# Routing attention and a tanh-shrink MLP on one core: the first batch's pairs readied two pairs ahead, the weight conversion in two stages, the up-projection handed out in single products

## The chip, the cores and the metric

The kernel runs on one core of a Trainium2 chip. The metric is the device time of one execution in microseconds (us), and for several executions their median.

## The reference

```python
# B=4 batches, H=8 heads, S=768, D=64, 16 clusters; d_model 512, d_ff 2048
q_assign = argmax(einsum('bhsd,hcd->bhsc', q_n, c_n))      # the same for k
mask = q_assign[:, :, :, None] == k_assign[:, :, None, :]
scores = where(mask, q @ k.T / sqrt(D), -1e9)
attn = softmax(scores) @ v
x = attn.transpose(0, 2, 1, 3).reshape(B * S, H * D)
h = x @ w_in
out = (h - tanh(h)) @ w_out
```

The weights arrive as float64. The kernel reads them as pairs of 32-bit words and makes float32 of them on the chip.

## The kernel before, in words

**Attention.** The heads are taken in pairs, four pairs to a batch, 16 pairs n = 0 to 15. A pair takes six steps (two halves of the queries, three slices of the keys each), so there are 96 steps, 24 to a batch. In the loop, step `at` issues `begin` of the step after it (score products, tile `sc`, L371, then the exponential on ACT, tile `e`) and `value` of its own (`av`, L424; in the first batch also the sums `den` by products with ones, L433). Everything else of the step is put on a list `todo`, which `between()` empties in pieces after each matrix product of the MLP.

**The mask.** Before a pair can begin, it must be readied (`before`, the table `PLACES`): `turn` (six transposes of q and six of k, `pt`, L264), `similar` (`sim`, L282), `route` (`pr`, L295, and four DVE instructions that find the cluster), `publish` (`pq`, L322, a copy `qc` on DVE, L326, and a DMA of the codes to DRAM), `spread` (a DMA that copies the codes to all partitions, tile `row`), and for pairs below `MASKED` = 4 `one_hot` (two DVE instructions, L352 and L356). For these pairs the mask is then added by four bf16 products a step (L382). For the others DVE selects by `e` = (row == code) * sc, four instructions a step (L402), which also free the score buffers. The readying of pair n stands in the six steps of pair n-1 and one before, at places -1, 0, 0, 2, 3, 4.

**The weights.** During the first batch the list `makers` is worked off: 32 pieces of 512 KB are fetched by POOL's queue (tile `raw`, five ahead), converted (`assemble`: one ACT instruction for the low words, tile `rest`, L136; three DVE instructions for the high words, L137, L141, L144, into tile `unit`), combined into the factors of a seven-product Strassen scheme (`sum_of`, L550), and written to DRAM (`keep`, tensors `up_factors` and `down_factors`). There are eight units of four pieces and four sums.

**The MLP.** Batch b's MLP (`strassen_items`) fills the steps of batch b+1; that of the last batch runs alone at the end. It has eight `up_pair` items (seven products each, tile `pu`, L649, with the additions to `G` and `u` on DVE, L634, tanh on ACT, and subtractions on POOL, L639) and 21 `down_product` items (tile `pd`, L693). An item is given a weight (9.1 and 3.4), and a step takes whole items until its share of the weight is reached.

Of the kernel before, what the change touches and what calls it, by code (L numbers as in the profile page):

```python
# [38 lines left out]
P = 128  # L39
# [13 lines left out]
MASKED = 4  # L53
# [5 lines left out]
def kernel(  # L59
# [67 lines left out]
    def assemble(dst, raw, rest):  # L127

        bits = dst.bitcast(U32)
        pair = raw.rearrange("p (n two) -> p n two", two=2)
        lo, hi = pair[:, :, 0], pair[:, :, 1]
        if len(dst.shape) == 3:
            lo, hi, rest = (t.rearrange("p (a b) -> p a b", a=dst.shape[1]) for t in (lo, hi, rest))
        nc.scalar.activation(out=rest, in_=lo, func=ACT.Copy, scale=2.0**-29)  # L136
        nc.vector.tensor_scalar(  # L137
            out=bits, in0=hi, scalar1=3, scalar2=0x3FFFFFF8,
            op0=ALU.logical_shift_left, op1=ALU.bitwise_and,
        )  # L140
        nc.vector.scalar_tensor_tensor(  # L141
            out=bits, in0=hi, scalar=0xC0000000, in1=bits, op0=ALU.bitwise_and, op1=ALU.bitwise_or
        )
        nc.vector.tensor_tensor(out=bits, in0=bits, in1=rest, op=ALU.add)  # L144

    def fast():
# [4 lines left out]
        codep = cx.enter_context(tc.tile_pool(name="codep", bufs=3))  # L151
# [12 lines left out]
        first, AHEAD = ExitStack(), 5  # L164
        xin = first.enter_context(tc.tile_pool(name="xin", bufs=HP))
        unitp = first.enter_context(tc.tile_pool(name="unitp", bufs=2))
        rawp = first.enter_context(tc.tile_pool(name="rawp", bufs=AHEAD))
        restp = first.enter_context(tc.tile_pool(name="restp", bufs=2))
# [90 lines left out]
        def turn(n: int, i: int, engine):  # L259
# [8 lines left out]
            t = turned[n, i] = turnp.tile([P, 2, TB], F32, name=f"t{i}")  # L268
# [63 lines left out]
        def spread(n: int):  # L332

            if masked(n):
                t = rows[n] = rowp.tile([P, 2, 2, TB], BF16, name="row")
# [5 lines left out]
            else:  # L341
                t = rows[n] = rowp.tile([P, 2, 2, TB], BF16, name="row")
# [149 lines left out]
        units = {}  # L492

        def sources(m: int):

            up, q_, r = m < HF // 2, m % 4 // 2, m % 2
            if up:
                t = units[m] = unitp.tile([P, FQ, 8, P], F32, name="unit")
# [5 lines left out]
            t = units[m] = unitp.tile([P, 8, 2, HM], F32, name="unit")  # L504
            made = []
            for o in range(2):
                f = q_ * FQ + 2 * r + o
                made.append((t[:, 0:8:7, o], w_out_r[:, f]))
                made.append((t[:, SLOT[2] : 7 : SLOT[3] - SLOT[2], o], w_out_r[:, f + HF]))
            return made  # L510

        raws, queue = {}, []

        def fetch(at: int):
            m, i = at // 4, at % 4
            if m >= 8:
                return
            if i == 0:
                queue.extend(sources(m))
# [6 lines left out]

        def round_piece(at: int):
            if words == 2:
                rest = restp.tile([P, FQ * P], U32, name="rest")
                assemble(queue[at][0], raws.pop(at), rest)  # L530
            fetch(at + AHEAD)

        def sum_of(m: int, k_: int):
            t = units[m]
            up = m < HF // 2

            def part(which):
                return t[:, :, which] if up else t[:, which]
# [6 lines left out]
                ) if up else (  # L545
# [6 lines left out]
        def keep(m: int):  # L552
            t, q_, r = units.pop(m), m % 4 // 2, m % 2
            if m < HF // 2:
# [4 lines left out]
            else:  # L559
                f = q_ * FQ + 2 * r  # L560
                nc.sync.dma_start(
                    down_factors[:, :, f : f + 2].rearrange("k p i m -> p k (i m)"),
                    t[:, 0:7].rearrange("p k i m -> p k (i m)"),
                )

        makers = []
        for m in range(8):
            makers += [lambda at=4 * m + i: round_piece(at) for i in range(4)]

            makers.insert(len(makers) - 2, lambda m=m: keep(m - 1) if m else None)  # L570
            makers += [lambda m=m, k_=k_: sum_of(m, k_) for k_ in range(4)]
        makers += [lambda: keep(7)]
# [15 lines left out]
        late_pools, diffs = {}, {}  # L588

        def open_late():  # L590
            first.close()
            for name, bufs in (
                ("diff", 1), ("u", 2), ("s", 2), ("th", 2), ("g", 1), ("left", 1), ("du", 1), ("c", 4),
                ("raw", 3),
            ):
                late_pools[name] = cx.enter_context(
                    tc.tile_pool(name=name + "_late", bufs=bufs, reuse_waits="tile")
                )
            late_pools["G"] = late_pools["g"].tile([P, HF, 2, 2, TB], F32, name="G")
            late_pools["S1"] = late_pools["left"].tile([P, HF, TB], F32, name="S1")  # L600
# [16 lines left out]
        def strassen_items(b: int):  # L617
            base = b * PER

            def up_pair(i: int, between):  # L620
# [7 lines left out]
                }  # L628
                s = late_pools["s"].tile([P, TB], F32, name="s")
                u = late_pools["u"].tile([P, 2, TB], F32, name="u")  # L630
                g, left1 = late_pools["G"][:, i], late_pools["S1"][:, i]
# [13 lines left out]
                for k_, which in enumerate(PRODUCTS):  # L645
                    ps = ps_f.tile([P, TB], F32, name="pu", tag="f")
                    for c in range(CH):
                        for r in halves:
                            nc.tensor.matmul(  # L649
                                ps[r], lhsT=streams[base + i][:, c, k_, r], rhs=right[which][c],  # L650
                                start=(c == 0), stop=(c == CH - 1),
                            )
                    if which == 1:
                        nc.scalar.copy(out=s, in_=ps)
                        fetch_factors(base + i + 2)
                    elif which == 2:
                        add(g[:, 0, 0], ps, s)
                    elif which == 6:
                        add(u[:, 0], ps, s)
                    elif which == 7:  # L660
                        add(u[:, 1], ps, u[:, 0])
                    elif which == 4:
                        add(g[:, 1, 0], ps, u[:, 1])
                    elif which == 5:
                        add(u[:, 0], ps, u[:, 0])
                        add(g[:, 1, 1], ps, u[:, 1])
                        shrink(1)
                    else:
                        add(g[:, 0, 1], ps, u[:, 0])
                        shrink(0)  # L670
                    between()

                nc.gpsimd.tensor_tensor(out=left1, in0=g[:, 0, 1], in1=g[:, 1, 1], op=ALU.add)
                nc.gpsimd.tensor_tensor(out=g[:, 0, 1], in0=g[:, 0, 0], in1=g[:, 0, 1], op=ALU.subtract)
                streams.pop(base + i)
# [136 lines left out]
        for i in range(AHEAD):  # L812
            fetch(i)
# [302 lines left out]
```

## Time and profile before

| what | value |
|---|---|
| median of 3 runs | 1080.9 us (1079.85 to 1081.64) |
| the profiled execution | 1073.9 us, span 1072.1 us |
| mean granted clock of TensorE | 0.979 of full speed |
| TensorE (PE) busy | 1001.2 us, 93% of the span |
| VectorE (DVE) busy | 604.1 us, 56% |
| GpSimd (POOL) busy | 571.7 us, 53% |
| ScalarE (ACT) busy | 297.2 us, 28% |

The time that the runs show is some 7 us above that of the profiled execution, so a difference that is worked out from the trace is put on the median as it is. PE is busy nearly all the time; the table does not show where it is not, nor where it is busy at half its clock.

### The profile page before, as it was taken

To read this page: it belongs to the slowest core of one execution; us is meant where nothing else is said; L and a number is where in the kernel's file an instruction comes from. 1 tells how busy PE (TensorE), PEld (TensorE's weight loads), DVE (VectorE), ACT (ScalarE), POOL (GpSimd) and SP (SyncE) were. 2 spreads that over 40 slices of the span, in tenths; PEclk is the share of its full clock that TensorE was granted. 3 is DMA by queue.
4 is the path that set the end of the run, shared out by engine and by line. 5 is a ranking of instruction groups with operands and counts; after the bars stand their busy time and mean duration, and the time that the engine had idled before them with its cause. 6 is when DMAs were issued, how large, how long until landed. Compare 5 with 4: busy or idle time off the path is not lost.

```text
span 1072.1 us, 17120 instructions
## 1 busy us (share of the span) xinstructions
PE 1001.2 (93%) x6820; PEld 500.3 (47%) x6820; DVE 604.1 (56%) x1103; ACT 297.2 (28%) x447; POOL 571.7 (53%) x423
## 2 busy tenths in 40 slices
PE   7986978998999999999999999999899999999996
PEld 5432433343445555434335555444345555444664
DVE  5767869666645556766556545755455544644011
ACT  2543434233232212332242222322332121122000
POOL 1111212575779545575768536576668645456701
PEclk8998989999999999999999999999999999999998
DMA  8756776444353534434353323313212212322320
GB/s 236 232 177 224 252 230 212 172 137 124 134 176 116 189 132 160 153 116 138 128 161 104 127 71 123 90 69 113 90 59 95 89 51 93 113 92 108 118 95 32
DMA packets 92183, 142.85 MB, mean 133 GB/s; under 512 B 55232, under 2 KB 63424, under 8 KB 88512
## 3 DMA queue, kind: packets, MB, share of 16 engines
q1 hardware_dynamic: 85040, 118.57, 33.8%
q0 software_dynamic: 6912, 23.07, 6.4%
q8 instruction: 56, 0.92, 0.3%
q14 instruction: 31, 0.25, 0.1%
q10 hardware_dynamic: 144, 0.03, 0.0%
HBM read 120.62 MB, written 21.03 MB: 132 GB/s over the span
## 4 chain that ended last, share of the span: by engine, by line
PE 66%; DVE 15%; issue 7%; DMA 6%; POOL 3%; ACT 2%; SPq 1%; POOLq 0%; DVEq 0%; ACTq 0%
PE pu L649 21%; PE pd L693 20%; PE sc L371 10%; PE av L424 9%; DMA row<-q_codes 3%; DVE e L402 2%; DVE den L466 2%; PE pt L264 2%; PE den L456 1%; DVE G L634 1%; PE sim L282 1%; DVE u L634 1%; DVE unit L550 1%; DMA x<-in_k_dram 1%; DMA q_codes<-qc 1%
## 5 line engine op out<-in xcount | busy, mean ns | idle before, releaser
L693 PE MATMUL pd<-stream,G 128*64 128x256 f32 x2304 | 256.9, 379 | 1.4 <-POOL G L639 1.4
L402 DVE SCALAR_TENSOR_TENSOR e<-row,code,sc 128x384 f32<-128x384 bf16 x288 | 160.5, 608 | 84.5 <-ACT sc L392 73.9
L693 PEld LDWEIGHTS pd<-stream,G 128*64 128x64 f32 x2304 | 164.5, 137 | 92.6 <-issue 12.5
L415 POOL TENSOR_TENSOR sum<-sum,e 128x768 f32<-128x768 f32 x96 | 174.6, 1818 | 42.0 <-DVE e L402 37.5
L649 PE MATMUL pu<-xT,stream 128*64 128x384 f32 x1024 | 181.4, 488 | 3.0 <-DVE u L634 1.6
L371 PE MATMUL sc<-t,t 64*128 64x384 f32 x768 | 155.0, 517 | 23.9 <-DVE e L402 20.7
L639 POOL TENSOR_TENSOR G<-G,th 128x768 f32<-128x768 f32 x64 | 115.5, 1826 | 99.3 <-ACT th L638 99.3
L392 ACT ACTIVATE sc<-sc 128x768 f32<-128x768 f32 x144 | 108.8, 788 | 188.5 <-PE sc L371 188.5
L424 PE MATMUL av<-e,vals 128*64 128x384 f32 x768 | 151.7, 518 | 0.0
L649 PE MATMUL pu<-diff,stream 128*64 128x384 f32 x768 | 135.0, 486 | 2.4 <-DVE G L634 2.1
L649 PEld LDWEIGHTS pu<-xT,stream 128*64 128x64 f32 x1024 | 72.2, 137 | 94.0 <-issue 83.7
L638 ACT ACTIVATE th<-G 128x768 f32<-128x768 f32 x64 | 52.9, 842 | 213.5 <-DVE G L634 212.8
L371 PEld LDWEIGHTS sc<-t,t 64*128 64x128 f32 x768 | 65.7, 186 | 98.1 <-issue 44.4
L649 PEld LDWEIGHTS pu<-diff,stream 128*64 128x64 f32 x768 | 54.8, 137 | 72.1 <-issue 64.4
L424 PEld LDWEIGHTS av<-e,vals 128*64 128x64 f32 x768 | 48.2, 141 | 85.5 <-issue 84.0
L466 DVE RECIPROCAL den<-den 128x128 f32<-128x128 f32 x96 | 84.2, 918 | 4.1 <-POOL wholes L461 4.1
L709 POOL DMA_DIRECT2D out_dram<-c x48 | 26.8, 557 | 107.3 <-DVE c L704 107.2
L470 POOL TENSOR_TENSOR inverses<-inverses,den 128x384 f32<-128x384 f32 x32 | 42.2, 1318 | 73.0 <-DVE den L466 71.7
L704 DVE TENSOR_TENSOR c<-pd,du 128x256 f32<-128x256 f32 x48 | 20.2, 422 | 102.5 <-PE pd L693 102.5
L634 DVE TENSOR_TENSOR G<-pu,u 128x384 f32<-128x384 f32 x96 | 52.5, 550 | 21.8 <-PE pu L649 21.5
L634 DVE TENSOR_TENSOR G<-pu,s 128x384 f32<-128x384 f32 x32 | 17.8, 557 | 77.8 <-PE pu L649 75.4
L411 POOL TENSOR_TENSOR sum<-e 128x768 f32<-128x768 f32 x24 | 43.6, 1815 | 33.2 <-DVE e L402 33.2
(98 smaller groups left out, 891.1 us busy)
## 6 DMA issues: line engine op xcount, KB each, us to landing
stream<-up_factors SPq DMA_DIRECT2D x32, 896.0 KB, 6.2
stream<-down_factors SPq DMA_DIRECT2D x28, 1024.0 KB, 5.9
raw<-in_moe_w_in_dram POOLq DMA_DIRECT2D x16, 512.0 KB, 6.2
raw<-in_moe_w_out_dram POOLq DMA_DIRECT2D x16, 512.0 KB, 5.3
again<-in_moe_w_in_dram SPq DMA_DIRECT2D x32, 256.0 KB, 2.9
again<-in_moe_w_out_dram SPq DMA_DIRECT2D x32, 256.0 KB, 5.1
up_factors<-unit SPq DMA_DIRECT2D x4, 1792.0 KB, 9.9
down_factors<-unit SPq DMA_DIRECT2D x4, 1792.0 KB
```

The source lines that it names most:

```text
L371: nc.tensor.matmul(sc[i][:, h, 0:TB], lhsT=turned[n, 1][r].rearrange("p a n -> p (a n)")[:, j * P : (j + 1) * P], rhs=turned[n, 0][r, half ...
L392: nc.scalar.activation(out=out, in_=sc[i][:, :, 0:TB], func=ACT.Exp, scale=SCALE)
L402: nc.vector.scalar_tensor_tensor(out=e[:, h], in0=rows[n][:, half, h], scalar=codes[n][:, 1, j // HCH, h, j % HCH : j % HCH + 1], in1=sc[: ...
L411: nc.gpsimd.tensor_tensor(out=s, in0=pair[:, 0], in1=pair[:, 1], op=ALU.add)
L415: nc.gpsimd.tensor_tensor(out=s, in0=s, in1=pair[:, i], op=ALU.add)
L424: nc.tensor.matmul(avs[n, half][h * D : h * D + D], lhsT=vals[n][:, h, j], rhs=e[:, i, h], start=(j == 0), stop=(j == NCH - 1),)
L466: nc.vector.reciprocal(out=t[:, c], in_=t[:, c])
L634: nc.vector.tensor_tensor(out=out, in0=x, in1=y, op=ALU.add)
L638: nc.scalar.activation(out=th, in_=g[:, f], func=ACT.Tanh)
L639: nc.gpsimd.tensor_tensor(out=g[:, f].rearrange("p a n -> p (a n)"), in0=g[:, f].rearrange("p a n -> p (a n)"), in1=th.rearrange("p a n -> ...
L649: nc.tensor.matmul(ps[r], lhsT=streams[base + i][:, c, k_, r], rhs=right[which][c], start=(c == 0), stop=(c == CH - 1),)
L693: nc.tensor.matmul(ps[r], lhsT=left[:, i, r], rhs=t[:, i], start=(i == 0), stop=(i == HF - 1))
```

## The change

- `MASKED` goes from 4 to 5: pair 4, the first of batch 1, is masked by products too.
- In the first batch (pairs 1 to 3) the readying stands one pair earlier. All of pair 1's is issued ahead of the loop, but for its `one_hot`, which is put at step 2. Pairs 2 and 3 are readied in the steps of pairs 0 and 1, at places 1, 2, 2, 4, 5, 7. From pair 4 on the places are the old ones. Pair 2 gets buffers of its own.
- The conversion is split: the low words of piece `at + 1` go to ACT when piece `at` is combined on DVE.
- The factors of `w_out` are made in eight units of two pieces instead of four of four, and `makers` ends six steps into batch 1 (`MADE`). One maker stands right behind the selection in each step's `todo`.
- The MLP's up-projection is handed out in 56 single products of weight 1.3 instead of eight groups of seven. `G` and the sums `S` are two tiles of four groups each; the second is opened when its first product is due (`open_rest`, which first empties `makers`), and the instructions on POOL that change all of `G` are halved.
- At the end, two and two products (not two and two groups) stand around the closing check.

```diff
-MASKED = 4
+MASKED = 5
...
+        def rest_of(at: int):
+            if words == 2 and at < PIECES:
+                rests[at] = restp.tile([P, FQ * P], U32, name="rest")
+                low_words(queue[at][0], raws[at], rests[at])
+
         def round_piece(at: int):
+            rest_of(at + 1)
             if words == 2:
-                rest = restp.tile([P, FQ * P], U32, name="rest")
-                assemble(queue[at][0], raws.pop(at), rest)
+                high_words(queue[at][0], raws.pop(at), rests.pop(at))
             fetch(at + AHEAD)
...
+        def open_rest():
+            while makers:
+                makers.pop(0)()
+            making.close()
+            open_pools("right", ("g1", 1), ("left1", 1), ("du", 1), ("c", 4), ("raw", 3))
+            of_half(1)
...
-            return [(9.1, 7, lambda between, i=i: up_pair(i, between)) for i in range(HF)] + [
+            return [
+                (1.3, 1, lambda between, i=i, k_=k_: up_product(i, k_, between))
+                for i in range(HF) for k_ in range(len(PRODUCTS))
+            ] + [
...
-        PLACES = (-1, 0, 0, 2, 3, 4)
         ready = {}
-        for n in range(1, len(pairs)):
+        for n in range(2, len(pairs)):
+            first_step, places = (n - 1, (-1, 0, 0, 2, 3, 4)) if n >= HP else (n - 2, (1, 2, 2, 4, 5, 7))
             for i, stage in enumerate(before(n)):
-                ready.setdefault((n - 1) * 2 * NS + PLACES[i], {})[i] = stage
+                ready.setdefault(first_step * 2 * NS + places[i], {})[i] = stage
...
+        turn(1, 0, nc.scalar)
+        turn(1, 1, nc.scalar)
         load(1, (2,))
         load(2)
+        similar(1)
+        rest_of(0)
+        makers.pop(0)()
+        route(1)
+        publish(1)
+        spread(1)
         load(3)
...
-        MADE = 2 * HALF
+        MADE = 2 * HALF + 2 * NS
...
+            if makers:
+                todo.append(makers.pop(0))
             todo += [stages[i] for i in (5, 2, 0) if i in stages]
...
             if makers:
-                share = -(-len(makers) // max(MADE - at, 1))
-                todo += makers[:share]
-                makers = makers[share:]
-            if late_pools:
+                share = -(-(len(makers) + 1) // max(MADE - at, 1))
+                todo += makers[: share - 1]
+                del makers[: share - 1]
+            if "raw" in late_pools:
                 todo += [check_done, check_done, check_on, check_on]
```

What stands on PE ahead of the first scores. Before, from pair 0's `pq` on (`x0_227` and `x1_230` are pair 1's q and k):

```order
L322 MATMUL pq_272<-ident_60,code_270 24x128
L264 MATMUL pt_296<-ident_60,x0_227 128x128 x6
L264 MATMUL pt_305<-ident_60,x1_230 128x128 x6
L235 MATMUL warm_335<-inverses_65 128x256 x6
L371 MATMUL sc_344<-t0_240,t1_249 128x384 x2
L371 MATMUL sc_347<-t0_240,t1_249 128x384 x2
```

In the change, from the same `pq` on:

```order
L333 MATMUL pq_281<-ident_60,code_279 24x128
L274 MATMUL pt_290<-ident_60,x0_233 128x128 x6
L274 MATMUL pt_299<-ident_60,x1_236 128x128 x6
L293 MATMUL sim_317<-t0_297,bd_64 32x384 x2
L293 MATMUL sim_317<-t1_306,bd_64 32x384 x2
L306 MATMUL pr_333<-ident_60,simt_322 128x128 x3
L333 MATMUL pq_344<-ident_60,code_342 24x128
L245 MATMUL warm_373<-inverses_65 128x256 x4
L382 MATMUL sc_380<-t0_249,t1_258 128x384 x2
```

Pair 1's `sim`, `pr` and `pq`, which stood among the steps of pair 0, now stand ahead of the first scores.

On DVE at the end of the first batch, before: the last conversion and sums, the selection for pair 4's first step (`e_1375`), and pair 3's division.

```order
L144 ISA unit_1061<-unit_1061,rest_1323 128x2x512
L550 TENSOR_TENSOR unit_1061<-unit_1061 128x512 x3
L402 SCALAR_TENSOR_TENSOR e_1375<-row_1289,code_1204,sc_1352 128x384 x2
L402 SCALAR_TENSOR_TENSOR e_1375<-row_1289,code_1204,sc_1355 128x384 x2
L466 RECIPROCAL den_1369<-den_1369 128x128 x3
L469 TENSOR_TENSOR xT_1273<-xT_1273,den_1369 128x384
L550 TENSOR_TENSOR unit_1061<-unit_1061 128x512
L611 TENSOR_TENSOR diff_1466<-xT_465 128x384
```

In the change, the same stretch:

```order
L567 TENSOR_TENSOR unit_991<-unit_991 128x256 x3
L363 TENSOR_SCALAR row_1280<-row_1280,mine_code_132 128x768
L367 TENSOR_SCALAR row_1280<-row_1280,mine_code_132 128x768
L144 TENSOR_SCALAR unit_1086<-raw_1087 128x2x256
L148 SCALAR_TENSOR_TENSOR unit_1086<-raw_1087,unit_1086 128x2x256
L151 ISA unit_1086<-unit_1086,rest_1272 128x2x512
L144 TENSOR_SCALAR unit_1086<-raw_1150 128x2x256
L148 SCALAR_TENSOR_TENSOR unit_1086<-raw_1150,unit_1086 128x2x256
L151 ISA unit_1086<-unit_1086,rest_1342 128x2x512
L477 RECIPROCAL den_1372<-den_1372 128x128 x3
L480 TENSOR_TENSOR xT_1259<-xT_1259,den_1372 128x384
```

Pair 4's selection is gone from DVE; its `one_hot` (`row_1280`) stands there instead, two steps ahead of the pair's first scores, and conversions are still to come.

On PE in batch 1, before: the end of one group, a step that has no product of the MLP, and the first of the next group.

```order
L649 MATMUL pu_1987<-xT_1273,stream_1694 64x384 x2
L371 MATMUL sc_2002<-t0_1389,t1_1398 128x384 x2
L371 MATMUL sc_2005<-t0_1389,t1_1398 128x384 x2
L424 MATMUL av_1913<-e_1928,vals_1372 64x384 x4
L322 MATMUL pq_2027<-ident_60,code_1956 12x128
L371 MATMUL sc_2033<-t0_1389,t1_1398 128x384 x2
L371 MATMUL sc_2036<-t0_1389,t1_1398 128x384 x2
L424 MATMUL av_1913<-e_2014,vals_1372 64x384 x4
L649 MATMUL pu_2049<-xT_465,stream_1808 64x384 x2
```

In the change, one step of that part and the next one's scores:

```order
L382 MATMUL sc_1896<-t0_1392,t1_1401 128x384 x2
L382 MATMUL sc_1899<-t0_1392,t1_1401 128x384 x2
L435 MATMUL av_1904<-e_1817,vals_1375 64x384 x4
L687 MATMUL pu_1931<-xT_502,stream_1694 64x384 x2
L687 MATMUL pu_1931<-xT_777,stream_1694 64x384 x2
L687 MATMUL pu_1942<-xT_1015,stream_1694 64x384 x2
L687 MATMUL pu_1942<-xT_1259,stream_1694 64x384 x2
L306 MATMUL pr_1952<-ident_60,simt_1894 128x128 x3
L687 MATMUL pu_1963<-diff_1465,stream_1694 64x384 x4
L687 MATMUL pu_1970<-xT_502,stream_1694 64x384 x2
L687 MATMUL pu_1970<-xT_777,stream_1694 64x384 x2
L382 MATMUL sc_1980<-t0_1392,t1_1401 128x384 x2
```

Where a step had seven products or none, each step now has four or five.

## Rows read from the trace of the kernel before

**Rows 1.** Waits of PE: engine, line, waited for; us in total, times, longest

```profile
PE sc L382 <- DVE row L356: 21.0, 4, 8.0
PE sc L371 <- DVE e L402: 20.7, 12, 3.0
PE pu L649 <- DVE G L634: 3.5, 2, 2.1
```

**Rows 2.** Chain that ended last, readying of pair 2: start, us, what

```profile
83.94 0.28 DVE qc L326
...
84.24 3.71 DMA q_codes<-qc
...
88.64 9.64 DMA row<-q_codes
```

**Rows 3.** PE in order of time, first batch: start, us, what [idle before]

```profile
27.40 0.50 PE L382 MATMUL sc<-row 64*128 64x384 bf16 x4 [1.02 <-DVE row L356]
...
75.81 0.28 PE L322 MATMUL pq<-ident,code 128*24 128x128 f32 x1
...
99.17 0.82 PE L382 MATMUL sc<-row 64*128 64x384 bf16 x4 [7.52 <-DVE row L356]
99.93 2.83 PE L424 MATMUL av<-e,vals 128*64 128x384 f32 x8
...
108.75 0.49 PE L382 MATMUL sc<-row 64*128 64x384 bf16 x4
109.17 1.51 PE L424 MATMUL av<-e,vals 128*64 128x384 f32 x8
...
117.14 1.56 PE L371 MATMUL sc<-t,t 64*128 64x384 f32 x8
...
121.69 1.56 PE L371 MATMUL sc<-t,t 64*128 64x384 f32 x8
```

**Rows 4.** Busy us by stretch: PE, PEld, DVE, ACT, POOL, then clock, DMA share, GB/s

```profile
58.20:99.20 41.00, 32.94 (x194) 14.12 (x195) 31.63 (x48) 17.43 (x27) 8.96 (x12) 0.92 0.61 212
...
26.60:185.50 158.90, 132.89 (x780) 56.75 (x782) 121.56 (x185) 70.10 (x108) 33.78 (x41) 0.94 0.68 220
...
200.00:316.00 116.00, 107.80 (x645) 46.08 (x643) 69.17 (x136) 41.32 (x61) 82.28 (x55) 1.00 0.45 140
316.00:440.00 124.00, 124.00 (x973) 70.02 (x971) 75.11 (x140) 27.43 (x42) 73.87 (x52) 1.00 0.45 150
440.00:562.00 122.00, 113.56 (x661) 47.94 (x659) 72.57 (x142) 41.42 (x61) 81.85 (x55) 0.97 0.41 133
...
680.00:806.00 126.00, 119.08 (x704) 50.67 (x702) 70.35 (x129) 42.05 (x62) 85.98 (x57) 0.99 0.24 80
```

**Rows 5.** PE in order of time, pair 5's transposes at the batch's end

```profile
180.13 0.84 PE L264 MATMUL pt<-ident,x 128*128 128x128 f32 x6 [2.59 <-issue]
```

**Rows 6.** DVE in order of time, the same place

```profile
178.90 2.18 DVE L402 SCALAR_TENSOR_TENSOR e<-row,code,sc 128x384 f32<-128x384 bf16 x4
```

**Rows 7.** DVE by line and shape up to 198 us: count, busy us, mean ns

```profile
L144 DVE CUSTOM_DVE_ANT_0 unit<-unit,rest 128x1024 uint16<-128x1024 uint16 x32 | 23.8, 743 | 20.2 <-ACT rest L136 16.1 <-DVE unit L141 0.6
L550 DVE TENSOR_TENSOR unit<-unit 128x512 f32<-128x512 f32 x32 | 22.5, 737 | 0.5
L141 DVE SCALAR_TENSOR_TENSOR unit<-raw,unit 128x512 uint32<-128x512 uint32 x32 | 22.2, 692 | 1.1
L137 DVE TENSOR_SCALAR unit<-raw 128x512 uint32<-128x512 uint32 x32 | 21.4, 667 | 0.4
...
L402 DVE SCALAR_TENSOR_TENSOR e<-row,code,sc 128x384 f32<-128x384 bf16 x8 | 4.4, 606 | 0.0
```

**Rows 8.** DVE in order of time, the closing check

```profile
933.31 1.79 DVE L913 TENSOR_SCALAR largest<-largest 128x16 f32<-128x16 f32 x1
```

**Rows 9.** POOL in order of time, the same moment

```profile
933.04 4.19 POOL L639 TENSOR_TENSOR G<-G,th 128x768 f32<-128x768 f32 x2 [3.33 <-ACT th L638]
```

**Rows 10.** Tile raw up to 200 us, its DMAs

```profile
DMA to landing us min/median/max: 3.5/6.0/9.9
```

More of the change, by code (lines that the diff above doesn't have):

```diff
@@ L125, in all_pieces, with shaped, low_words, high_words @@
         ]
-    def assemble(dst, raw, rest):
-        bits = dst.bitcast(U32)
[L132 to L136, printed above, removed]
+    def shaped(dst, raw, rest):
+        pair = raw.rearrange("p (n two) -> p n two", two=2)
+        parts = pair[:, :, 0], pair[:, :, 1], rest
+        if len(dst.shape) == 3:
+            parts = (t.rearrange("p (a b) -> p a b", a=dst.shape[1]) for t in parts)
+        return parts
+    def low_words(dst, raw, rest):
+        lo, _, rest = shaped(dst, raw, rest)
+        nc.scalar.activation(out=rest, in_=lo, func=ACT.Copy, scale=2.0**-29)
+    def high_words(dst, raw, rest):
+        _, hi, rest = shaped(dst, raw, rest)
+        bits = dst.bitcast(U32)
         nc.vector.tensor_scalar(
@@ L618, in strassen_items, with up_product @@
             base = b * PER
-            def up_pair(i: int, between):
+            held = {}
+            def up_product(i: int, k_: int, between):
+                if b == 0 and i == HF // 2 and k_ == 0:
+                    open_rest()
+                which = PRODUCTS[k_]
                 x = [xT[b * HP + c] for c in range(CD)]
@@ L643, in shrink @@
                     )
[L645 to L671, printed above, removed]
@@ L673, in up_pair @@
-                nc.gpsimd.tensor_tensor(out=left1, in0=g[:, 0, 1], in1=g[:, 1, 1], op=ALU.add)
-                nc.gpsimd.tensor_tensor(out=g[:, 0, 1], in0=g[:, 0, 0], in1=g[:, 0, 1], op=ALU.subtract)
-                streams.pop(base + i)
+                ps = ps_f.tile([P, TB], F32, name="pu", tag="f")
+                for c in range(CH):
+                    for r in halves:
+                        nc.tensor.matmul(
+                            ps[r], lhsT=streams[base + i][:, c, k_, r], rhs=right[c],
+                            start=(c == 0), stop=(c == CH - 1),
+                        )
@@ new lines, in up_product @@
+                if which == 1:
+                    nc.scalar.copy(out=s, in_=ps)
+                    fetch_factors(base + i + 2)
+                elif which == 2:
+                    add(g[:, 0, 0], ps, s)
+                elif which == 6:
+                    add(u[:, 0], ps, s)
+                elif which == 7:
+                    add(u[:, 1], ps, u[:, 0])
+                elif which == 4:
+                    add(g[:, 1, 0], ps, u[:, 1])
+                elif which == 5:
+                    add(u[:, 0], ps, u[:, 0])
+                    add(g[:, 1, 1], ps, u[:, 1])
+                    shrink(1)
+                else:
+                    add(g[:, 0, 1], ps, u[:, 0])
+                    shrink(0)
@@ L712, in down_product @@
                     put(0, 0, u[:, 0])
-                    nc.gpsimd.tensor_tensor(out=a12, in0=a12, in1=a11, op=ALU.subtract)
+                    for a in range(2):
+                        a12 = gs[a][:, :, 1, 0, c]
+                        nc.gpsimd.tensor_tensor(
+                            out=a12, in0=a12, in1=gs[a][:, :, 0, 0, c], op=ALU.subtract
+                        )
                 elif which == 6:
@@ L834, in fast @@
             select(*steps[0][:2], i)
+        ready[2] = {**ready.get(2, {}), 5: lambda: one_hot(1)}
         fills = {2 * (b + 1) * HALF: b for b in range(B - 1)}
-        MADE = 2 * HALF
+        MADE = 2 * HALF + 2 * NS
         late, divides = [], []
@@ L950, in general @@
             rest = gs.tile([P, FQ * P], U32, name="grest")
-            assemble(dst, raw, rest)
+            low_words(dst, raw, rest)
+            high_words(dst, raw, rest)
             nc.vector.tensor_scalar(
```

153 lines of the change are left out of this document (87 added, 66 removed).

## The prediction

> **What bounds the kernel now.** The table gives PE 93% of the span, so I read first what PE waits for [rows 1] and then its busy time and clock by stretches [rows 4]. Two places come out. In the first batch PE waits 21.0 us for L356, the second half of `one_hot`, four times, up to 8.0 us each. One of the four is the kernel's start (1.02 us before the mask at 27.40); the other three, 20.0 us, are the arrivals of pairs 1 to 3 [rows 1, 3]. In batches 1 to 3 it waits 20.7 us, twelve times, for L402, the selection on DVE. The stretches show that these lie in the up-projections alone: PE is busy 107.80 of 116, 113.56 of 122 and 119.08 of 126 us there, and 124.00 of 124 in the down-projection between the first two [rows 4]. So PE idles 8.2 + 8.4 + 6.9 = 23.6 us in the three up-projections and not at all where the MLP comes in single products.
>
> Why a pair is late is in the chain that ended last [rows 2]. For pair 2, PE has the codes ready at 75.81 + 0.28 = 76.1 us [rows 3]; the copy `qc` starts at 83.94, 7.9 us later, behind conversions and sums in DVE's queue; then the codes take 3.71 us to DRAM and 9.64 us back to all partitions, and the mask starts at 99.17. That is 23 us, and the order gives PE about 15 us of other work (its wait was 7.52).
>
> **The change, part by part.** Durations are those of the profiled execution (1073.9 us, span 1072.1); the difference is put on the median of 1080.9.
>
> 1. *Pairs 1 to 3 readied two pairs ahead.* From `spread` to `one_hot` there are now two steps and to the pair's first scores six or seven, of 4.55 us each (117.14 to 121.69 in [rows 3]). The 23 us of the chain fit into that twice. The three waits go: **-20.0**. Behind each wait PE ran slow: the mask took 0.82 instead of 0.49 us and `av` 2.83 instead of 1.51 [rows 3], at a mean granted clock of 0.92 over that pair [rows 4], part of it at the lower of the two levels. That is 1.65 us a wait: **-5.0**. Pair 1's products ahead of the loop are hidden by the wait for pair 0's own row: 0, at most +2.
>
> 2. *Pair 4 masked, with the old places.* Its codes are published at place 2, its `one_hot` is at 4 and its scores at 5, as for pairs 1 to 3 before. So it takes over their fate: a wait of 7.5 us if DVE's queue is as long as then. In front of its `qc` stands about one conversion less (2.1 us by [rows 7]) and sums half as wide, and the factors' write ahead of it in SP's queue is half as big; I take 4 us, with 0.8 us of slow clock behind it, between 0 and 9. Against that, two waits go. Pair 5's transposes waited 2.59 us at 180.13 for score buffers that DVE's selection freed late, from 178.90 on [rows 5, 6]; with the mask, ACT frees them. And of the 3.5 us for `G` [rows 1], all but the longest (2.1, in the closing check) goes, 1.4 us: it was the first addition of batch 1, whose buffer lay where the last unit still was on its way to DRAM. That wait can come back at `open_rest`, hidden by three product buffers. Sum: **+0.8**. The mask's products cost 0.42 us a step (108.75 to 109.17, [rows 3]) in six steps: **+2.5**.
>
> 3. *What the first batch must now do in less time.* From 26.6 to 185.5 us DVE is busy 121.6 of 158.9 us and the DMA engines 0.68 of it, 108 us [rows 4]. A conversion is 0.667 + 0.692 + 0.743 = 2.1 us on DVE [rows 7]. Four of them leave the batch (-8.4), four selections of 0.606 go (-2.4). The sums were 32 of 0.737 and are 16 such and 22 of half the width; a half one lies between 0.37 and 0.74, so they change by -3.6 to +4.4. DVE then has about 111 us in 158.9 - 20.0 - 5.0 + 0.8 = 135 us, 0.82; the transfers are all but the same, so DMA's share is 0.80. Neither is the bound, but both are fuller, and the conversion's ACT instruction now reads its raw piece one piece earlier: **+3**, between 0 and 10.
>
> 4. *Up-projection in single products.* Each step has four or five, 5 to 6 us, between one selection and the next scores. The 23.6 us of waits should go as they are gone in the down-projection. The clock of 0.97 and 0.99 in two of the stretches is worth up to 122 x 0.03 + 126 x 0.01 = 4.9 us more. DVE still has steps with a routing and a division, and POOL is busy 82.28 of 116 us, so I leave 5 us of the waits and 2 of the clock: 18.6 + 3 = **-21.6**, between 0 and -28.5.
>
> 5. *Makers in batch 1.* Four conversions and ten half sums (13 us on DVE, with 0.45 for a half sum) move into six steps that lose 24 selections (14.5 us), so DVE's load stays. But POOL is busy there 0.71 of the time, against 33.78 of 158.9 us in the first batch [rows 4], and the two engines get in each other's way: an instruction of 16 columns took 1.79 us on DVE while POOL worked two instructions off in 4.19 us [rows 8, 9]. The 22 instructions each wait up to the 1.8 us of such an instruction; at 0.71 and half of it, 14 us of DVE. PE has three product buffers in front of it: **+1.5**, between 0 and 10.
>
> The Trainium skill has this as a rule (SBUF — State Buffer, section "Who interferes with whom"): a VectorE instruction with two SBUF inputs or in its two-port mode and a GpSimd instruction that reads SBUF shut each other out for the whole instruction. By that rule the trace agrees, and it speaks against moving two-input sums beside a busy GpSimd; it is a rival below.
>
> 6. *The rest.* POOL's instructions on all of `G` are halved in size and doubled in number, off PE's path while products remain. In the closing check two products stand in front instead of fourteen; POOL then has no subtraction to block DVE, but PE's transpose comes earlier. The 2.1 us stay: 0.
>
> Sum: -20.0 - 5.0 + 0.8 + 2.5 + 3 - 21.6 + 1.5 = -38.8. The profiled execution would come to 1035, the median to **1042 us**, 3.6% less.
>
> **The rivals.**
>
> - *The transfers stay the limit.* If the DMA engines cannot do their 108 us in less than now, parts 1 to 3 give nothing and only 4 and 5 and the mask remain: -21.6 + 1.5 + 2.5, 1063 us. For it: the row's 9.64 us and 0.61 to 0.68 of all engines busy [rows 2, 4]. Against: raw pieces land in 6.0 us at the median and 9.9 at most [rows 10], with steps of 4.55 us and five pieces ahead.
> - *The up-projection's waits move.* The selection shares DVE with eight additions a group, and POOL's subtractions with its row sums; if each step is a little late instead of each third one much, part 4 gives nothing: 1042 + 21.6 = 1064 us. Against it is the down-projection's 124.00 of 124, though DVE has fewer additions there.
> - *DVE and POOL shut each other out in the first steps of batch 1* (the rule above): the 14 us of DVE reach PE but for what the buffers hide, 10 us instead of 1.5: 1051 us.
> - *No friction:* the upper bounds of all gains, pair 4 in time, nothing lost in 3 and 5: -20.0 - 5.0 - 4.0 + 2.5 - 28.5 = -55: 1026 us.
> - *Slower:* the exponentials wait behind the low words. ACT's conversion instruction stands in its queue ahead of later exponentials, and now needs its raw piece four pieces after the fetch instead of five, some 18 us at a step each. If pieces land later than that, every exponential behind waits, and PE with it. To eat the 38.8 us, 25 pieces would each have to hold ACT by 1.6 us, so land after 19.6 us on the mean: twice the longest and three times the median of [rows 10]. Beyond that it is slower than 1083.
>
> **How the numbers follow.** Chances: 0.64 for the forecast (its own range, from the bounds of 2, 3 and 4, is 1031 to 1054), 0.10 for the transfers, 0.12 for moved waits, 0.04 for the shut-out, 0.06 for no friction, 0.04 for slower. The range from 1024 to 1060 holds the first, fourth and fifth case (0.74) and about half of those at 1063 and 1064, whose gains would come in part. A change of under 0.2% (2.2 us) cannot be told from none by these runs; it needs the second and third case together, 0.02, which is taken from them. Slower is the last case, 0.04; faster is the rest, 0.94.
>
> **What would show it.** In the profile after: no waits for L367 (`one_hot`'s new line) at pairs 1 to 3, at most one, at pair 4; the first `pu` product near 167 instead of 187.6 us; PE's clock at 1.00 through the first batch but for pair 4; waits of `sc` for the selection (L413) far under 20.7 us; PE busy all through the up-projections; in the first 55 us of batch 1, L567 at up to 1.8 us where POOL is busy. The prediction is wrong if `row` lands after its two steps and DVE waits for it, if waits for `pr` or `pq` come in their place, or if ACT waits for `raw`.

## The result and the profile after

The changed kernel takes 1036.49 us (median of 4 runs, 1034.88 to 1036.94) against 1080.38 us of the kernel before beside it (1077.77 to 1081.64): a ratio of 0.9594, 95% interval 0.9573 to 0.9615, so 4.1% faster. The forecast was 1042, the range 1024 to 1060. Profiled execution against profiled execution it is 1036.4 against 1073.9, -37.5 us, where the steps summed to -38.8.

The page of the kernel after, share of each engine and the chain that ended last:

```profile
PE 993.4 (96%) x6840; PEld 498.7 (48%) x6840; DVE 608.5 (59%) x1101; ACT 297.4 (29%) x447; POOL 575.8 (56%) x447
...
PE 78%; DVE 11%; issue 6%; POOL 3%; ACT 1%; POOLq 0%; DVEq 0%; ACTq 0%
```

DMA, 6% of the chain before, is gone from it. Waits of PE after (engine, line, waited for; us in total, times, longest):

```profile
PE pq L333 <- DVE code L319: 5.5, 2, 3.0
PE sc L382 <- ACT e L403: 4.8, 5, 1.9
PE pt L274 <- issue: 2.9, 8, 0.5
PE pu L687 <- DVE diff L641: 2.9, 3, 1.5
...
PE pu L687 <- DVE qc L337: 1.8, 1, 1.8
```

Both great rows of [rows 1] are gone. No wait for the selection (now L413) is left, and of the 21.0 us for `one_hot` (now L367) one wait of 1.23 us, at pair 4. A new row has come: the exponentials (L403), 4.8 us.

Busy time by stretch of the kernel after: first batch, then the up-projections of batches 1 to 3 (PE, PEld, DVE, ACT, POOL, clock, DMA share, GB/s):

```profile
26.90:165.60 138.70, 131.47 (x799) 57.40 (x800) 109.55 (x173) 69.08 (x105) 34.59 (x43) 0.98 0.78 246
...
165.60:295.10 129.50, 121.77 (x722) 51.53 (x720) 90.22 (x143) 42.90 (x65) 86.83 (x56) 0.99 0.40 128
...
412.70:531.70 119.00, 116.98 (x706) 50.71 (x704) 78.02 (x152) 41.37 (x61) 84.83 (x56) 1.00 0.44 145
...
649.30:768.30 119.00, 116.99 (x707) 50.72 (x705) 72.39 (x132) 41.34 (x61) 84.83 (x56) 1.00 0.26 87
```

PE is busy 0.95 of the first batch and 0.98 of the up-projections of batches 2 and 3, but idles 7.7 of 129.5 us in batch 1. By PE's order of time, from the first product `pu` to the first `pd`, the up-projections took 128.4, 129.5 and 126.6 us before; now they take 129.5, 119.0 and 119.0. The first `pu` starts at 165.57 instead of 187.63. So the first batch gave 22.1 us, batches 2 and 3 gave 18.1, and batch 1 gave nothing, though its waits for the selection are gone. The three down-projections between take 0.7 us more each than before (117.6, 117.6 and 108.2 against 116.9, 116.9 and 107.5), and from the last batch's first `pu` to the end it is 0.8 us less; with these the parts add up to the 37.8 us between the spans, 1072.1 and 1034.3.

What stands there instead is in DVE's and POOL's order of time, first steps of batch 1:

```profile
186.42 1.44 DVE L144 TENSOR_SCALAR unit<-raw 128x512 uint32<-128x512 uint32 x1
187.89 2.19 DVE L148 SCALAR_TENSOR_TENSOR unit<-raw,unit 128x512 uint32<-128x512 uint32 x1
190.12 2.19 DVE L151 CUSTOM_DVE_ANT_0 unit<-unit,rest 128x1024 uint16<-128x1024 uint16 x1
```

```profile
187.54 4.23 POOL L426 TENSOR_TENSOR sum<-sum,e 128x768 f32<-128x768 f32 x2
```

The two instructions of a late maker that take two inputs in SBUF last 2.19 us each; together they fill 187.89 to 192.31, beside POOL's two sums at 187.54 to 191.77. By DVE's lines and shapes, L151 takes 692 ns in the first batch and 1442 in the first 60 us of batch 1:

```profile
L151 DVE CUSTOM_DVE_ANT_0 unit<-unit,rest 128x1024 uint16<-128x1024 uint16 x26 | 18.0, 692 | 3.4
...
L151 DVE CUSTOM_DVE_ANT_0 unit<-unit,rest 128x1024 uint16<-128x1024 uint16 x4 | 5.8, 1442 | 0.2
```

### The profile page after: what moved, and what is told of

It is laid out like the page before. It is cut to its first block, busy times and chain, and to the rows that moved or that the text cites. A ratio compares the mean times of both kernels' runs of the same rounds, so it can differ in the third digit from the quotient of the medians.

```text
span 1034.3 us, 17189 instructions
## 1 busy us (share of the span) xinstructions
PE 993.4 (96%) x6840; PEld 498.7 (48%) x6840; DVE 608.5 (59%) x1101; ACT 297.4 (29%) x447; POOL 575.8 (56%) x447
## 4 chain that ended last, share of the span: by engine, by line
PE 78%; DVE 11%; issue 6%; POOL 3%; ACT 1%; POOLq 0%; DVEq 0%; ACTq 0%
PE pu L687 27%; PE pd L736 20%; PE sc L382 11%; PE av L435 11%; PE pt L274 2%; DVE den L477 2%; PE sim L293 2%; PE den L467 2%; DVE unit L151 2%; DVE unit L148 1%; DVE unit L567 1%; DVE unit L144 1%; PE den L444 1%; PE warm L245 1%; POOL G L678 1%
## 5 line engine op out<-in xcount | busy, mean ns | idle before, releaser
L736 PEld LDWEIGHTS pd<-stream,G 128*64 128x64 f32 x2304 | 164.5, 137 | 94.6 <-issue 12.3
L413 DVE SCALAR_TENSOR_TENSOR e<-row,code,sc 128x384 f32<-128x384 bf16 x264 | 146.9, 606 | 49.8 <-ACT sc L403 49.8
L403 ACT ACTIVATE sc<-sc 128x768 f32<-128x768 f32 x132 | 98.8, 791 | 219.0 <-PE sc L382 214.0
L382 PE MATMUL sc<-t,t 64*128 64x384 f32 x768 | 151.9, 515 | 4.8 <-ACT e L403 4.8
L435 PE MATMUL av<-e,vals 128*64 128x384 f32 x768 | 145.4, 500 | 0.0
L687 PE MATMUL pu<-diff,stream 128*64 128x384 f32 x768 | 137.8, 488 | 5.0 <-DVE diff L641 2.9
L403 ACT ACTIVATE e<-sc 128x768 f32<-128x768 f32 x60 | 45.2, 806 | 55.0 <-PE sc L393 55.0
L472 POOL TENSOR_TENSOR wholes<-wholes,den 128x384 f32<-128x384 f32 x32 | 32.4, 1011 | 38.3 <-ACT den L471 38.2
```

The lines of the kernel that those rows point to most:

```text
L382: nc.tensor.matmul(sc[i][:, h, 0:TB], lhsT=turned[n, 1][r].rearrange("p a n -> p (a n)")[:, j * P : (j + 1) * P], rhs=turned[n, 0][r, half ...
L403: nc.scalar.activation(out=out, in_=sc[i][:, :, 0:TB], func=ACT.Exp, scale=SCALE)
L413: nc.vector.scalar_tensor_tensor(out=e[:, h], in0=rows[n][:, half, h], scalar=codes[n][:, 1, j // HCH, h, j % HCH : j % HCH + 1], in1=sc[: ...
L435: nc.tensor.matmul(avs[n, half][h * D : h * D + D], lhsT=vals[n][:, h, j], rhs=e[:, i, h], start=(j == 0), stop=(j == NCH - 1),)
L687: nc.tensor.matmul(ps[r], lhsT=streams[base + i][:, c, k_, r], rhs=right[c], start=(c == 0), stop=(c == CH - 1),)
L736: nc.tensor.matmul(ps[r], lhsT=left(i)[:, r], rhs=t[:, i], start=(i == 0), stop=(i == HF - 1))
```

## Experiments

One table holds all runs. "First `pu`" is the start of batch 1's first product in PE's order of time, "up 1 to 3" the us from there, and from its likes in batches 2 and 3, to the first `pd`, both worked out from starts rounded to 0.1 us, so a difference of 0.1 says nothing. "Span" is that of the profiled execution. The ratio is to runs of the kernel before beside each.

| kernel | median us | ratio, 95% interval | span | first `pu` | up 1 | up 2 | up 3 |
|---|---|---|---|---|---|---|---|
| before | 1080.38 | 1 | 1072.1 | 187.6 | 128.4 | 129.5 | 126.6 |
| changed | 1036.49 | 0.9594 (0.9573 to 0.9615) | 1034.3 | 165.6 | 129.5 | 119.0 | 119.0 |
| e1 up in groups | 1065.18 | 0.9881 (0.9838 to 0.9923) | 1065.2 | 166.0 | 139.9 | 132.2 | 127.1 |
| e2 readied late | 1046.62 | 0.9713 (0.9673 to 0.9753) | 1043.9 | 176.7 | 128.0 | 119.0 | 119.0 |
| e3 makers in first batch | 1040.74 | 0.9654 (0.9621 to 0.9688) | 1039.3 | 178.2 | 121.9 | 119.0 | 119.0 |
| e4 before + singles | 1052.12 | 0.9767 (0.9732 to 0.9802) | 1049.8 | 189.7 | 120.9 | 118.9 | 119.0 |
| e5 e3 + third buffer | 1036.39 | 0.9611 (0.9583 to 0.9640) | 1035.2 | 172.1 | 123.6 | 119.0 | 119.0 |
| e6 no sums on POOL | 1027.45 | 0.9531 (0.9496 to 0.9565) | 1024.8 | 163.9 | 121.7 | 119.0 | 119.0 |
| e7 four masked | 1032.86 | 0.9583 (0.9552 to 0.9614) | 1032.8 | 164.5 | 128.5 | 119.0 | 118.9 |
| e8 not split | 1031.98 | 0.9565 (0.9533 to 0.9597) | 1030.3 | 159.7 | 131.3 | 118.9 | 119.0 |
| e9 e7 + e8 | 1029.80 | 0.9534 (0.9506 to 0.9563) | 1028.7 | 159.1 | 130.0 | 118.9 | 118.9 |
| e10 e9 + e3 | 1031.80 | 0.9555 (0.9528 to 0.9582) | 1029.4 | 169.7 | 120.2 | 119.0 | 119.0 |
| e11 e9, makers half way | 1034.22 | 0.9576 (0.9549 to 0.9603) | 1032.3 | 169.6 | 123.2 | 119.0 | 119.0 |
| e12 third buffer | 1029.90 | 0.9537 (0.9511 to 0.9564) | 1028.2 | 159.5 | 129.5 | 119.0 | 118.9 |

The runs stand in groups (before and changed; e1 to e4; e5 to e8; e9 to e11; e12), each beside its own runs of the kernel before, whose medians were 1080.38, 1077.56, 1076.90, 1081.16 and 1080.84 us. So the medians of two groups can lie some 4 us apart with nothing changed, and "less" or "more" than the changed kernel is safe by the medians only where the interval of the ratio lies outside the changed kernel's (e1, e2, e3, e6, e9 and e12; e4 is set against the kernel before). For the others (e5, e7, e8, e10, e11) the spans and the stretches of the traces carry the argument.

My theory after the result was: each part does its own work, and the late makers lose batch 1's gain to POOL. The rival for batch 1 was the length of DVE's queue, whoever is beside it; that for the first batch was that one part alone gave its 22 us.

**e1.** The up-projection again in groups of seven:

```diff
-                (1.3, 1, lambda between, i=i, k_=k_: up_product(i, k_, between))
-                for i in range(HF) for k_ in range(len(PRODUCTS))
+                (9.1, 7, lambda between, i=i: [up_product(i, k_, between) for k_ in range(len(PRODUCTS))])
+                for i in range(HF)
```

> The changed kernel with one edit undone: the up-projection is handed out again in groups of seven products, the rest stays. If the single products, spread evenly, took the waits of the up-projection away (step 4 of the prediction), batches 2 and 3 go back to up-projections of about 126 to 129 us instead of 119, and batch 1 loses little, since it gained nothing: 15 to 20 us slower, 1052 to 1056. If the waits had gone for another reason (the earlier readied pairs, a changed order on VectorE), the time stays at 1035 to 1038.

Measured: 1065.18, 28.7 us more, not 15 to 20. The waits for the selection are back, and batch 1 loses 10.4 us too. Waits of PE in e1:

```profile
PE sc L382 <- DVE e L413: 18.5, 10, 3.0
PE sc L382 <- ACT e L403: 7.5, 5, 2.0
```

So the singles gain in batch 1 as well; the late makers only hide it.

**e2.** Pairs 1 to 3 readied at their places of before:

```diff
-        for n in range(2, len(pairs)):
-            first_step, places = (n - 1, (-1, 0, 0, 2, 3, 4)) if n >= HP else (n - 2, (1, 2, 2, 4, 5, 7))
+        for n in range(1, len(pairs)):
+            first_step, places = n - 1, (-1, 0, 0, 2, 3, 4)
```

> The changed kernel with pairs 1 to 3 readied at their places of before, the rest stays. If the earlier readying gave the first batch its 22 us (step 1), the waits for the broadcast row come back in pairs 1 to 3 and the first product of the up-projection goes from 165.6 us to 187 to 190: 20 to 25 us slower, 1057 to 1061. If the split of the conversion gave a part of it, less comes back: 5 to 15 us slower, with the waits shorter than the 13.7, 7.6 and 4 us of before.

Measured: 1046.62, 10.1 us more, half of what was expected: the first `pu` goes to 176.7, not to 187. The row of waits is back (PE in e2):

```profile
PE sc L393 <- DVE row L367: 17.9, 5, 6.1
```

But 5.72 of the 17.9 us are the kernel's start and 1.23 are pair 4. Pairs 1 to 3 wait 4.20, 6.06 and 0.72 us, 11.0 together:

```profile
58.95 0.82 PE L393 MATMUL sc<-row 64*128 64x384 bf16 x4 [4.20 <-DVE row L367]
...
99.36 0.82 PE L393 MATMUL sc<-row 64*128 64x384 bf16 x4 [6.06 <-DVE row L367]
...
134.35 0.50 PE L393 MATMUL sc<-row 64*128 64x384 bf16 x4 [0.72 <-DVE row L367]
```

Before, they waited 4.52, 7.52 and 7.96 us, 20.0 together (not the 13.7, 7.6 and 4 of the expectation). So the readying is not the whole of the 22 us: the other parts of the change had taken 9 us off the same waits by themselves, most of it at pair 3. From its `pq` to its `one_hot` 16.5 us pass in e2 (117.00 to 133.48) and 23.0 before (116.93 to 139.93); the DMAs of the row land in 7.9 us at the median against 9.3. Whether the missing makers or the half-wide units did this, e2 does not separate.

**e3.** The makers end with the first batch, as before:

```diff
-        MADE = 2 * HALF + 2 * NS
+        MADE = 2 * HALF
```

> The changed kernel with the makers of w_out's factors ending with the first batch, as before the change, the rest stays. Theory: in the first steps of batch 1 these makers stand beside GpSimd's subtractions, take 2.19 us for 0.69 each, and hold up VectorE's queue; without them the waits between 186 and 220 us go and batch 1's up-projection falls from 129.5 to 121 to 125 us, while VectorE in the first batch (0.79 of it busy) takes the 10 us more without a wait: 3 to 8 us faster, 1028 to 1033. Rival: the first batch has no room, its waits come back (for the selection, for the row): the up-projection starts 3 to 10 us later and the time is 1034 to 1042.

Measured: 1040.74, 4.3 us more; the rival holds for the first batch, the theory for batch 1. The first `pu` comes 12.6 us later, and batch 1's up-projection falls to 121.9 us. The two stretches of e3:

```profile
26.90:178.20 151.30, 134.99 (x797) 59.25 (x799) 119.00 (x195) 70.61 (x108) 34.48 (x43) 0.95 0.75 238
...
178.20:300.10 121.90, 118.85 (x723) 51.62 (x721) 69.77 (x121) 41.23 (x62) 84.40 (x56) 1.00 0.38 118
```

Against the changed kernel 22 instructions of DVE move from batch 1 into the first batch. There they add 119.00 - 109.55 = 9.5 us of DVE; in batch 1 they were 90.22 - 69.77 = 20.5 us. PE in the first batch now waits for exponentials, three times more than 4 us:

```profile
65.80 2.85 PE L382 MATMUL sc<-t,t 64*128 64x384 f32 x8 [4.28 <-ACT e L403]
```

**e4.** The kernel before with the single products alone, that is with the part of the diff that turns `up_pair` into `up_product`, on whole tiles `G` and `S1`.

> The kernel before with the single products of the up-projection alone. If this part stands by itself and has nothing to do with the others, it gives some 17 us in batches 2 and 3 and, as no maker of w_out's factors stands in batch 1, another 3 to 8 us there: 18 to 25 us faster than before, 1055 to 1062. If it needs the earlier readied pairs, less than 10 us.

Measured: 1052.12, 25.4 us less than before beside it (1077.56), just past the 18 to 25 expected; 22.3 by the profiled spans. As expected, batch 1's up-projection falls too, to 120.9 us. The part stands by itself.

**e5.** e3 with `restp` of three buffers instead of two (room is made by one constant's tile that serves twice).

> The changed kernel with the makers ending with the first batch and with a third buffer for the low words. Theory: in the first batch ScalarE's low words wait for a buffer that VectorE must free, and the exponentials queued behind them come 4.3 to 4.5 us late, three times; a third buffer lets ScalarE pass, so the first batch ends 5 to 10 us sooner than with the makers ending there alone (168 to 173 us instead of 178.2), batch 1 keeps its 121.9 us: 1030 to 1036. Rival: VectorE itself or the transfers set the pace of the first batch (0.79 and 0.75 busy); the waits move to other rows and the time stays at 1038 to 1042.

Measured: 1036.39, 4.3 us less than e3, with the first `pu` at 172.1. The first batch ends 6.1 us sooner, as the theory had it, but batch 1 takes 123.6 us, and the total stays just above its range. Waits for exponentials of 2.25 and 6.26 us stay in PE's order of time; before the second, ACT's low words stand 5.08 us behind L151 in spite of the third buffer, so DVE is late there as well.

**e6.** POOL's sums left out for pairs 4 and 5 but for the first of each half (the denominators lack that part):

```diff
-                else:
+                elif n not in (4, 5):
                     s = sums[n, half]
```

> The changed kernel without GpSimd's sums of the weights for the first two pairs that run in batch 1, but for the first of each half (this part of the softmax denominators is left out): some 30 us of GpSimd's work less in the 60 us in which the late makers stand. If GpSimd's work blocks VectorE there, the makers' 2.19 us instructions fall back to 0.69 us at the places of the sums, the waits at 193.7 and 214 to 217 us shrink, and batch 1's up-projection takes 123 to 127 us instead of 129.5: 3 to 6 us faster, 1030 to 1034. If it is the length of VectorE's own queue, the waits stay and the time is 1035 to 1038.

Measured: 1027.45, 9.0 us less, more than the 3 to 6 expected. DVE has the same 143 instructions in batch 1's up-projection, yet is busy 8.6 us less, and PE takes 121.7 us, about as in e3 (121.9) where no maker stands there. Stretch of e6, and L151 in its first 60 us of batch 1:

```profile
163.90:285.60 121.70, 119.23 (x722) 51.46 (x720) 81.65 (x143) 43.00 (x65) 57.62 (x40) 1.00 0.44 137
```

```profile
L151 DVE CUSTOM_DVE_ANT_0 unit<-unit,rest 128x1024 uint16<-128x1024 uint16 x4 | 3.5, 863 | 0.2
```

So the makers cost PE little in batch 1 by themselves; what costs is POOL beside DVE. Of PE's waits in the changed kernel those for `u` and `G` (1.22 and 1.18 us, at 214.45 and 217.15) are gone, and the one for `qc` is 1.03 us instead of 1.83; this last is what stays of the queue's length as a rival. But not all of the gain is the makers': the two waits for `diff` (1.46 and 1.04 us, at 169.78 and 171.69) go as well, and e3 keeps them (1.34 and 1.04 us). They hang on subtractions of two inputs in SBUF (L641), which POOL's sums held up too: the four of `diff<-xT,diff` take 926 ns in the mean, and 554 in e6. So e6 and e3 come to the same time in part by accident.

**e7.** `MASKED = 4`.

> The changed kernel with only the first four pairs masked by a product, as before. By step 2 of the prediction the wait on the score buffers (2.59 us) and the one for the first sum (1.5 us) come back and the six steps of mask products (2.5 us) go, with the row's wait of 1.23 us: 0 to 2 us slower, 1036 to 1039. Rival: the selections on VectorE then stand beside the late makers and GpSimd in batch 1's first steps and hold up the products of the up-projection: 4 to 10 us slower.

Measured: 1032.86, 3.6 us less by the medians, 1.5 by the profiled spans; neither theory had it faster. By the ratios e7 cannot be told from the changed kernel; the 1.5 us come again between e8 and e9 (spans 1030.3 and 1028.7). Of the 2.59 us of [rows 5] only 0.86 come back.

**e8.** The split undone: `round_piece` calls `rest_of(at)`, and no piece is begun ahead.

> The changed kernel with both stages of a conversion in one piece again: ScalarE's low words are no longer made one piece ahead. If the split is worth what VectorE waits for low words less (16.1 us before, 4.1 us after, not on TensorE's path), 0 to 2 us slower, 1036 to 1039. If the split gave a good part of the first batch's 22 us, 5 us slower or more. If the lead costs more than it gives, since ScalarE waits for VectorE with 24.5 us instead of 9.8, 1 to 3 us faster.

Measured: 1031.98, 4.5 us less (4.1 by the spans): the third case, above its size. The first `pu` comes 5.9 us sooner, and no wait for exponentials of 0.8 us or more is left.

**e12.** The split kept, `restp` with three buffers (room is made as in e5):

```diff
-        restp = making.enter_context(tc.tile_pool(name="restp", bufs=2, side="right"))
+        restp = making.enter_context(tc.tile_pool(name="restp", bufs=3, side="right"))
```

> The changed kernel, split kept, with a third buffer for the low words. If what the split costs is that ScalarE, one piece ahead, waits for a buffer which VectorE has still to read, with the exponentials behind it, the three waits for them in the first batch (3.8 us together) go and the first batch ends at 160 to 162 us instead of 165.6: 1031 to 1034, as without the split. If the lead itself is what costs (ScalarE's work comes at the wrong place), the waits stay: 1035 to 1038.

Measured: 1029.90, 6.6 us less (6.1 by the spans), the waits gone. The cause is thus the buffer, not the lead, which with a third buffer is worth some 2 us (span 1028.2 against 1030.3 in e8). How it reached PE in the changed kernel shows in order of time: DVE's last conversion instruction ends, ACT's low words start, the exponentials follow, and PE has stood still.

```profile
67.18 0.69 DVE L151 CUSTOM_DVE_ANT_0 unit<-unit,rest 128x1024 uint16<-128x1024 uint16 x1
...
67.91 0.67 ACT L139 ACTIVATE rest<-raw 128x512 uint32<-128x512 uint32 x1 [2.48 <-DVE unit L151]
68.47 1.49 ACT L403 ACTIVATE e<-sc 128x768 f32<-128x768 f32 x2
...
69.32 2.54 PE L382 MATMUL sc<-t,t 64*128 64x384 f32 x8 [1.93 <-ACT e L403]
```

ACT's waits for that buffer from 26 to 166 us, changed kernel (the first of its nine, 4.65 us, ends before the first scores) and then e12:

```profile
ACT rest L139 <- DVE unit L151: 24.3, 9, 4.7
```

```profile
ACT rest L139 <- DVE unit L151: 7.2, 5, 2.2
```

**e9, e10, e11.** e9 is e7 and e8 together; e10 has e3's `MADE` as well, e11 `MADE = 2 * HALF + NS` (three steps into batch 1: the last sum of a maker starts at 200.6 us, in the changed kernel at 227.7).

> The changed kernel without the split of the conversion and with four pairs masked by a product. The two savings of 4.5 and 3.6 us stand in different places (ScalarE's queue in the first batch; TensorE's mask products at its end): if they are independent they add, 1027 to 1030. If both give back the same time (both leave ScalarE's exponentials sooner or later in the same steps), 1031 to 1033.

> As the run with both undone, and the makers end with the first batch. If the 12.6 us that these makers cost in the first batch were the exponentials behind ScalarE's low words, they are mostly gone without the split: the first batch ends at 162 to 166 us, batch 1 takes 122 us, 1020 to 1026. If VectorE's work sets the pace there, the first batch ends at 169 to 173 us: 1028 to 1033.

> The same with the makers ending three steps into batch 1, half of the way. If the costs on both sides grow evenly, the time lies between those with the makers at either place; if either side has some room (the first batch takes a few makers for nothing, or the first steps of batch 1, with little of GpSimd's work, do), it is 1 to 4 us below the better of the two.

Measured: e9 1029.80, 6.7 us less than the changed kernel, a little under the sum of 8.1; by the spans it is 5.7, and 1.6 + 4.1 = 5.7, so the two are independent. e10 1031.80: the first batch ends at 169.7, the second theory's value, with two waits for exponentials of 3.57 and 4.73 us even without the split, and batch 1 gives 9.8 us back. e11 1034.22 is worse than either: the first batch loses 10.5 us like e10, and batch 1 wins 6.8. So the first batch does not take this part of the makers for nothing, and the one middle that was tried does not pay. e9 and e12 are the best kernels found that leave nothing out, equal within their intervals, which also touch those of e8 and e10; a third buffer with four masked pairs was not tried.

## Why the prediction was right, and where its terms were not

The sum was right within 1.3 us of the profiled executions (-38.8 against -37.5), by errors of both signs: step 1 is too large by more than 10 us, and what the makers' absence gives the first batch, which no step counted as time, fills that gap. That it came out so close is luck.

1. **Pairs 1 to 3 (-25).** The waits went as said, and the first `pu` came at 165.57, near the 167 forecast. But only 10.1 us hang on the readying alone (e2). The step took the waits of [rows 1] as its own. In fact the makers in that batch held the same stretch, and the two parts add: the earlier readying moves the first `pu` by 11.5 us with the makers there (189.7 to 178.2, e4 to e3, which also differ by the split, the mask and the half units) and by 11.1 with them gone (176.7 to 165.6, e2 to the changed kernel). One of the signs of being wrong came, at a small price: pair 1's `pq` waits 2.99 us for `code` ahead of the loop, and the first mask comes at 29.20 us instead of 27.40 (26.20 in e2), within the +2 that the step allowed.

2. **Pair 4 (+0.8 and +2.5).** Its wait was 1.23 us, not 4. The total of +3.3 lies between e7's 1.5 (spans) and 3.6 us (medians). What it was to take away had shrunk: 0.86 us for the score buffers in e7, not 2.59.

3. **Friction (+3).** Measured: 4.5 (e8) to 6.6 us (e12). The prediction looked at when the raw piece is there; ACT has no wait for that in the changed kernel. The buffer of the low words was short: with a lead of one piece and two buffers, ACT waits for DVE's previous piece, 24.3 us in nine waits, with exponentials behind it. It is the slower rival's queue with another releaser, at a small part of that rival's price.

4. **Single products (-21.6).** Right in kind, and by the spans in size: -22.3 alone (e4; -25.4 by the medians), 28.7 back when undone beside the late makers (e1), and -10.5 and -7.6 us in the up-projections of batches 2 and 3. With batch 1's 7.5 the three up-projections of e4 give 25.6 us of the upper bound of 28.5; the down-projections, 0.7 us longer each, take 2.1 of that back, and the first batch ends 2.1 us later.

5. **Makers in batch 1 (+1.5).** This step failed on both sides. DVE's extra was estimated at 14 us and measured 20.5 - 9.5 = 11.0, but the three product buffers did not hide it: 7.6 us reach PE (129.5 against 121.9 us, e3): by the stretches it idles 4.7 us more and is busy 2.9 us longer. The makers' absence in the first batch was worth 12.6 us there (178.2 to 165.6), which the step did not count. Net it is a gain of 4.3 us (5.0 by the spans). Part of the loss is the clock: behind the waits for `diff` eight products take 2.78 us, where sixteen took 2.75 just before, so PE runs at the lower of its two levels (1.2 GHz) for a few us; the granted clock is 0.95 in the first 34 us of batch 1. What brings it down stays open: e3 has two such waits (1.34 and 1.04 us), yet eight products behind them take 1.46 us, and 1.00 is granted. The changed kernel:

```profile
165.57 2.75 PE L687 MATMUL pu<-xT,stream 128*64 128x384 f32 x16
169.78 0.87 PE L687 MATMUL pu<-diff,stream 128*64 128x384 f32 x4 [1.46 <-DVE diff L641]
171.69 1.13 PE L687 MATMUL pu<-diff,stream 128*64 128x384 f32 x4 [1.04 <-DVE diff L641]
172.60 2.78 PE L687 MATMUL pu<-xT,stream 128*64 128x384 f32 x8
...
165.60:200.00 34.40, 30.07 (x174) 12.28 (x170) 27.32 (x38) 9.40 (x15) 16.91 (x10) 0.95 0.34 103
```

   The shut-out was named as a rival at 0.04, with 10 us in place of 1.5. Its mechanism is what happened, near its size (e6); only the other terms kept the total where the forecast had it, which is the luck named above. The Trainium skill (SBUF — State Buffer, section "Who interferes with whom") says that a VectorE instruction with two SBUF inputs and a GpSimd instruction that reads SBUF lock each other out. With it the trace agrees: L151 takes 0.69 us in the first batch, 2.19 beside POOL's sums, and 863 instead of 1442 ns in the mean once these are gone.

6. **The rest (0).** The tail is the same within 0.8 us (first `pu` of the last stretch 913.44 to 876.45, end of the span 1072.1 to 1034.3), and the closing check's 2.1 us went, but a wait of 1.43 us for its own last value (`pl`, L993) came.

The prediction's own range, 1031 to 1054, does not come out of the bounds of its steps 2 to 4, which add up to some 1028 and 1076; the sum does not use it.

From the sum to the median: the forecast added the 7 us by which the runs of before lie above their profiled execution. The changed kernel's profiled execution (1036.4) lies on its median, so the medians differ by 43.9 us. How long a run of before takes goes with the clock: beside e9, the shortest of 11 runs had 1072.72 us at a granted clock of 0.982, the longest 1083.99 at 0.971; e12's six go from 1028.52 at 0.996 to 1030.31 at 0.992. That the waits make this spread is not shown: e3, with three waits of over 4 us in its first batch, spreads by 1.2 us over four runs, and e9, with none of 1 us there, by 4.3 over six.

## What to carry to other kernels

When work leaves a full stretch, price what it frees there and what it meets where it goes: here the same 22 instructions were 9.5 us of VectorE in one place and 20.5 in the other. Waits that show on one row may be held by a second cause just behind; only undoing each part alone told 10 from 22 us. An instruction issued one piece ahead may need a buffer more: here its engine stood 24.3 us behind VectorE with two buffers, with exponentials queued behind it, and 7.2 us with three. And sort a row of waits by place before saying that it is back: here a third of it was the kernel's start.

## What was not expected of the hardware

Leaving out 29 us of GpSimd's work off the critical path made the kernel 9.0 us faster (e6; POOL busy 57.62 instead of 86.83 us in that stretch). VectorE had the same 143 instructions there and was busy 8.6 us less, and the waits of PE that went or shrank were all for VectorE.
